# Linear attention and MLP on one core: k normalized inside its exponential, one ring of PSUM banks, casting loads for batch 0, earlier loads for the rest

## The chip, the cores and the metric

The kernel runs on one core of one Trainium2 chip. The metric is the time of one execution in microseconds on the device. Executions of one kernel mostly agree within 0.3%. A program on one core has no second die to compare with, so a run is called slow only when it lies over 1.5% above the fastest of the same kernel.

Names: PE is TensorE, PEld its weight loads, DVE is VectorE, ACT is ScalarE, POOL is GpSimd, SP is SyncE, which only issues transfers here. L599 is line 599 of that kernel's file, so line numbers differ between kernels.

## The reference

Attention with random features over 8 batches, 8 heads, 576 rows and head size 64, then an MLP over the 4608 rows:

```python
def phi(x):                                   # x is q or k, scaled by 64 ** -0.25
    proj = np.einsum('bhsd,md->bhsm', x, omega)
    h = proj - np.sum(x * x, axis=-1, keepdims=True) / 2.0
    h = h - np.max(h, axis=-1, keepdims=True)
    return np.exp(h) / np.sqrt(m)
kv = np.einsum('bhsm,bhsd->bhmd', k_p, v)
z = np.sum(k_p, axis=2)
out = np.einsum('bhsm,bhmd->bhsd', q_p, kv) / (np.einsum('bhsm,bhm->bhs', q_p, z)[..., None] + 1e-06)
# ... out to rows of 512, then
g = h * np.clip(h + 3.0, 0.0, 6.0) / 6.0      # h = x @ w_in   (512 x 2048)
return g @ w_out                              # 2048 x 512
```

The square term cancels inside the maximum. For q the maximum cancels in the division too. For k it does not: each row of k has to be weighted by exp(-its maximum).

## The kernel before

A small scheduler in the file decides, when the program is built, the order of the operations on every engine. It simulates the engines with a cost per operation (`occ`) that the author wrote in, takes the operations by priority, and then emits each engine's list with semaphore waits. At run time every engine executes its list in order. Two of the costs are

```python
    def actt(n):                  # ScalarE, n columns
        return 0.07 + n / 1200.0

    def dvet(n):                  # VectorE
        return 0.07 + n / 960.0
```

The MLP of block b-1 is placed beside the attention of batch b, so that TensorE always has large matmuls to do. The k side of the attention, for each of nine groups of four 128-column chunks per batch:

```python
            op("ACT", actt(512), lambda E, u=u, vK=vK: E.activation(
                kp[pb][:, 4 * u:4 * u + 4, :].rearrange("p c m -> p (c m)"), ring.t[vK.slot], AF.Exp, scale=alpha),
               pos(u) + 0.02, reads=[vK], writes=[("kp", pb, u)], name="eK%d.%d" % (b, u))
            op("DVE", dvet(512), lambda E, u=u: E.reduce_max(
                mx[pb][:, 4 * u:4 * u + 4], kp[pb][:, 4 * u:4 * u + 4, :], axis=AX.X),
               pos(u) + 0.03, reads=[("kp", pb, u)], writes=[("mx", pb, u)], name="mx%d.%d" % (b, u))
```

One exponential covers 512 columns. The maximum is taken from the result, its reciprocal `cc` is the row's weight, and v is multiplied by it (`vc`, and `vcl` for the left-over rows 512 to 575). The kv matmuls follow:

```python
        cbc = bass.AP(cc[pb], c0, [[NCH, 128], [1, 8], [0, D]])
        # ...
        op(EV_V if b else V0, {"POOL": 1.2, "DVE": dvet(512)}, lambda E: E.tensor_tensor(
            vcm[:, :, 0:D], v32[:, m, :, :], cbc, ALU.mult),
           t, reads=[("cc", pb, m), ("v32", 0, m), ("v32", 1, m)], writes=[("vc", u2, 0)], name="vc" + nm)
```

Two of the eight PSUM banks are kept for the numerators, six go round in a ring:

```python
    num_ps = P8[:, 0:2, :]
    ring = Ring([P8[:, i, :] for i in range(2, 8)])
```

Batch 0 is loaded in fp32 through SP and ACT and cast on the engines; later k and q are cast by the transfer itself, issued from POOL. Loads of batches 3 to 7 start at given steps of the MLP (16 steps per block):

```python
            load(0, ("SP", "ACT", "SP", "ACT"), {t: [] for t in "kqv"})
            # ...
            load(b, (), {"k": [("m1", b - 2, 10)], "q": [("m1", b - 2, 13)], "v": [("m1", b - 2, 15)]})
```

The softmax here doesn't subtract the row's maximum and nothing guards it: scores larger than these inputs give would overflow.

Of the kernel before, what the change touches and what calls it, by code (L numbers as in the profile page):

```python
# [13 lines left out]
EV0 = (("ACT","DVE"), ("ACT","DVE"), ("POOL","DVE"), {"k": ("POOL", "ACT", "DVE"), "q": ("POOL", "ACT","DVE")})  # L14
# [284 lines left out]
def _emit(nc, es, q, k, v, omega, w_in, w_out, out):  # L299
# [6 lines left out]
    NP = H // 2  # L306
# [8 lines left out]
    SPLIT = 3  # L315
    LATE = 0.4
    FIRST = [("k", 1), ("q", 1), ("k", 0), ("v", 0), ("v", 1), ("q", 0)]
    REST = [("k", 1), ("k", 0), ("q", 1), ("q", 0), ("v", 0), ("v", 1)]
    W_GATE = [("v32", 0, 1), ("v32", 0, 3), ("v32", 1, 3), ("v32", 1, 3)]
    alpha = float(D) ** -0.25  # L320
    PE_T, PE_X = 2, 2
    SPARE = 1
    EV_T = ("DVE", "ACT")
    EV_C = ("POOL", "ACT", "DVE")
    EV_V = ("POOL", "DVE")
    EV_L = ("POOL", "ACT")
    K0, T0, V0, C0 = EV0
# [9 lines left out]
    k32 = sbt("k32", [128, NCH, D], F32)  # L337
    q32 = sbt("q32", [128, NCH, D], F32)
    v32 = sbt("v32", [128, NP, 8, D], F32)
    vl = [sbt("vl%d" % u, [128, NP, D + 1], F32) for u in range(2)]  # L340
    kb = sbt("kb", [128, NCH, D], BF16)
    qb = sbt("qb", [128, NCH, D], BF16)
    half = k32[:].rearrange("p c d -> p (c d)").bitcast(BF16)
    KB = [kb, half[:, 0:NCH * D].rearrange("p (c d) -> p c d", d=D)]
    QB = [qb, half[:, NCH * D:2 * NCH * D].rearrange("p (c d) -> p c d", d=D)]
# [5 lines left out]
    cc = [sbt("cc%d" % u, [128, NCH], F32) for u in range(2)]  # L351
    vc = [sbt("vc%d" % u, [128, 520], BF16) for u in range(2)]
# [13 lines left out]
    om = sbt("om", [128, 2, M], BF16)  # L366
    ident = sbt("ident", [128, 128], BF16)
    ones = sbt("ones", [128, 8], F32)

    P8 = es.enter_context(nc.psum_tensor("p8", [128, 8, 512], F32))  # L370
    num_ps = P8[:, 0:2, :]
    ring = Ring([P8[:, i, :] for i in range(2, 8)])
# [36 lines left out]
    def turned(vx, b, n):  # L409
# [5 lines left out]
    op("POOL", 0.3, lambda E: E.memset(ident[:], 0.0), -9, writes=["ident"], lat=0.1)  # L415
    op("POOL", 0.4, lambda E: E.affine_select(out=ident[:], in_=ident[:], compare_op=ALU.not_equal, fill=1.0,
                                              base=0, pattern=[[-1, 128]], channel_multiplier=1),
       -9, reads=["ident"], writes=["ident"])
    op("DVE", 0.1, lambda E: E.memset(om[64:128, 0, :], 0.0), -9, writes=["omz0"])
    op("DVE", 0.1, lambda E: E.memset(om[0:64, 1, :], 0.0), -9, writes=["omz1"])  # L420
    for u in range(2):
        op("DVE", 0.2, lambda E, u=u: E.memset(vcl[u][:], 0.0), -8, writes=[("vcz", u)])
        op("DVE", 0.1, lambda E, u=u: E.memset(vl[u][:, :, D:D + 1], 1.0), -8, writes=[("vl1", u)])
    op("DVE", 0.1, lambda E: E.memset(ones[:], 1.0), -8, writes=["ones"])
    for i in range(2):
        op("DVE", 0.15, lambda E, i=i: E.tensor_copy(om2[:, i, :], om32[:]), -9, reads=["om32"],
           writes=[("om2", i)])
# [4 lines left out]
    op("DVE", 0.2, lambda E: E.tensor_copy(om[0:64, 0, :], ring.t[vom.slot][0:64, 0:M]), -9, reads=[vom],  # L432
       writes=["om0"])
    op("DVE", 0.2, lambda E: E.tensor_copy(om[64:128, 1, :], ring.t[vom.slot][64:128, 0:M]), -9, reads=[vom],
       writes=["om1"])
    omk = ["om0", "om1", "omz0", "omz1"]

# [4 lines left out]
    def w_in_piece(i, gate):  # L442
        f0, f1 = WI[i]
        op("POOL", 0.9 * (f1 - f0), lambda E: E.dma_start(
            wi[:, :, 128 * f0:128 * f1], w_in[:, 128 * f0:128 * f1].rearrange("(c p) f -> p c f", p=128)),
           -8.6 + 0.05 * i, reads=gate, writes=[("wi", i)], group="dwi%d" % i, inc=16, lat=2.0, name="wi%d" % i,
           issue=0.85, packet=91.0)

    def w_out_piece(g, gate):
        op("POOL", 3.6, lambda E: E.dma_start(  # L450
# [8 lines left out]
    def load(b, eng, gates):  # L459
        pb = b % 2  # L460
        halves = HALVES if b == 0 else [(0, NP)]
        turn_of = [0]

        def dma(part, dst, src, n, keys, gate, prio, run):
            cast = b > 0 and part[0] in "kq"
            e = "POOL" if cast else eng[turn_of[0]] if turn_of[0] < len(eng) else "SP"
            op(e, n * (0.78 if run == 1024 else 1.15) / 262144.0 * (1.08 if cast else 1.0),
               lambda E: E.dma_start(dst, src), prio + 0.001 * turn_of[0], reads=gate + (free if cast else []), writes=keys,  # L468
               group="d" + part + ("c" if cast else "") + (str(pb) if b and part != "v" else ""), inc=16, lat=1.9,
               name="%s.%d" % (part, b), issue=0.85 if cast else 0.47, packet=50.0 if run == 1024 else 18.0)  # L470
            turn_of[0] += 1


        free = [("kb", 0, x) for x in range(NDC)] if b == 1 else []

        def landing(t, hh, m0, m1):

            if t == "v" or b == 0:
                return [(t + "32", hh, m) for m in range(m0, m1)]
            return [(t + "b", pb, 2 + 4 * m + 2 * hh + x) for m in range(m0, m1) for x in range(2)]  # L480
# [3 lines left out]
        def mains(t, src, dst):  # L484
            for x, (m0, m1) in enumerate(halves):
# [7 lines left out]
        def lefts_of(t, hh):  # L493
            return [(t + "b", pb, x, hh) for x in range(2)]

        def lefts(t, src, dst):
            if t == "q":
                for hh in range(2):
                    dma("ql%d" % hh, dst[64 * hh:64 * hh + 64, 0:NP, :],
                        src[b, hh:H:2, MAIN:S].rearrange("m s d -> s m d"), 65536, [("q32l", hh)] if b == 0 else lefts_of(t, hh),  # L500
                        gates[t], base[t], 256)
            else:
                sap = src[b].rearrange("(m h) s d -> m (h s) d", h=2)[:, MAIN:MAIN + 128, :]
                dma(t + "l", vl[pb][:, :, 0:D] if t == "v" else dst[:, 0:NP, :],
                    sap.rearrange("m x d -> x m d"), 131072, [("vl", pb)] if t == "v" else [("k32l", 0)] if b == 0 else lefts_of(t, 0),
                    gates[t], base[t], 256)

        tensors = {"k": (k, KB[pb] if b else k32), "q": (q, QB[pb] if b else q32), "v": (v, v32)}
        for t, part in FIRST if b == 0 else REST:
            (mains if part else lefts)(t, *tensors[t])  # L510


    def attention(b):
# [7 lines left out]
        def left_keys(t):  # L521
            return [(t + "32l", hh) for hh in range(2 if t == "q" else 1)]

        def main_keys(t, ms, hs=(0, 1)):
            return [(t + "32", hh, m) for m in ms for hh in hs]

        def rows_of(t, dbl):

            if b == 0:
                return [(t + "b", 0, x) for x in dbl]  # L530
# [8 lines left out]

        def cast(t, name, n, dst, src, rd, dbl, p):  # L540
            op(EV_C if b else C0[t], {"POOL": 0.1 + n / 850.0, "ACT": actt(n), "DVE": 0.1 + n / 1500.0}, evac(lambda: dst, lambda: src),
               p, reads=rd, writes=[(t + "b", 0, x) for x in dbl], name="cast%s%d.%s" % (t, b, name))
# [25 lines left out]
        def pairs(t):  # L568
            return t[:, NP:, :].rearrange("p (j s c) d -> p j s (c d)", s=2, c=2)

        if b == 0:
            for m0, m1 in HALVES:
                for hh in range(2):
                    nm = "%d%d" % (m0 // 2, hh)
                    dbl = four(m0, m1, hh)
                    cast("k", nm, 512, mains_of(kb)[:, m0:m1, hh, :], mains_of(k32)[:, m0:m1, hh, :],
                         main_keys("k", range(m0, m1), [hh]), dbl, 0)
                    turns("k", nm, dbl, dbls(kT)[:, m0:m1, hh, :], kb, 0)
            for s in range(2):
                for m0, m1 in HALVES:  # L580
                    nm = "%d%s" % (m0 // 2, "AB"[s])
                    dbl = every(m0, m1, s)
                    cast("q", nm, 512, pairs(qb)[:, 2 * m0:2 * m1, s, :], pairs(q32)[:, 2 * m0:2 * m1, s, :],
                         main_keys("q", range(m0, m1)), dbl, 0)
                    turns("q", nm, dbl, alts(qT, s, m0, m1), qb, 0)
            for t, src, cst, dst in (("k", k32, kb, kT), ("q", q32, qb, qT)):
                late = 0 if t == "k" else LATE
                cast(t, "l", 256, flat(cst[:, 0:NP, :]), flat(src[:, 0:NP, :]), left_keys(t), [0, 1], late)
                turns(t, "l", [0, 1], dst[:, 0:2, :], cst, late)
# [4 lines left out]
        else:  # L594
            for t, cst, dst in (("k", KB[pb], kT), ("q", QB[pb], qT)):
                for i, (x0, x1) in enumerate(((0, 10), (10, 18))):
                    op("SP", 0.21 * (x1 - x0), lambda E, x0=x0, x1=x1, cst=cst, dst=dst: E.dma_start_transpose(
# [4 lines left out]
        for u in range(NU):  # L602
            vK = Virt(ring)

            def e_K(E, u=u, vK=vK):
                for i in range(2):
                    ins = E.matmul(ring.t[vK.slot][:, 256 * i:256 * i + 256], kT[:, 2 * u + i, :],  # L607
                                   om[:].rearrange("d t m -> d (t m)"), start=True, stop=True)
                return ins

            op("PE", 2 * mmt(256), e_K, pos(u) + 0.02, reads=[("kT", 2 * u), ("kT", 2 * u + 1)] + omk, writes=[vK],
               alloc=[vK], lat=0.25, slack=sl, spare=sp, name="K%d.%d" % (b, u))
            op("ACT", actt(512), lambda E, u=u, vK=vK: E.activation(  # L613
                kp[pb][:, 4 * u:4 * u + 4, :].rearrange("p c m -> p (c m)"), ring.t[vK.slot], AF.Exp, scale=alpha),
               pos(u) + 0.02, reads=[vK], writes=[("kp", pb, u)], name="eK%d.%d" % (b, u))
            op("DVE", dvet(512), lambda E, u=u: E.reduce_max(  # L616
                mx[pb][:, 4 * u:4 * u + 4], kp[pb][:, 4 * u:4 * u + 4, :], axis=AX.X),
               pos(u) + 0.03, reads=[("kp", pb, u)], writes=[("mx", pb, u)], name="mx%d.%d" % (b, u))
# [345 lines left out]
```

## Time and profile before

| | before |
|---|---|
| time, median of the 4 runs beside the changed kernel | 329.75 us (329.56 to 330.75) |
| span of the profiled run | 328.2 us |
| PE busy | 313.8 us, idle 14.4 us |
| first MLP matmul | 21.78 us |
| first MLP matmul of block 1 | 62.98 us |
| last matmul ends | 324.1 us |

A busy engine is one whose instructions cover the time. For PE this flatters: a 512-column matmul is shown as 379 ns long although four in a row take 0.86 us, that is 216 ns from start to start. A gap of up to 0.16 us between two matmuls is therefore hidden in "busy". The prediction below shows the rows of the page.

### The profile page before, as it was taken

How to read it: one execution, taken by the hardware profiler on the slowest of the kernel's cores; microseconds unless marked ns; L12 is line 12 of the kernel's file. 1: busy time of each engine (PE TensorE's matmuls, PEld its weight loads, DVE VectorE, ACT ScalarE, POOL GpSimd, SP SyncE). 2: the span in 40 equal slices, each digit the busy share in tenths (PEclk: the TensorE clock that was granted, in tenths of full speed). 3: DMA queues.
4: the chain of work that ended last, by engine and by line, in shares of the span. 5: the costliest groups of instructions: out<-in, count | busy, mean ns of one | idle time of the engine just before them, and what ended most of it. 6: DMA issues, size and time to landing. Idle time of an engine off the chain costs nothing.

```text
span 328.2 us, 5706 instructions
## 1 busy us (share of the span) xinstructions
PE 313.8 (96%) x2185; PEld 168.8 (51%) x2185; DVE 213.8 (65%) x421; ACT 181.6 (55%) x372; POOL 76.2 (23%) x108
## 2 busy tenths in 40 slices
PE   3699999999999999999999999999999999999994
PEld 2367865554655544545645544556545444444442
DVE  3858977489596951798768814986878373443311
ACT  3776975288696530796756403984686164344400
POOL 2835525008223230072130600361310000000000
PEclk9989999999999999999999999999999999999999
DMA  7999999959993299659890999099802101000033
GB/s 254 228 194 155 235 178 153 298 109 106 214 216 94 38 163 252 175 61 142 181 244 18 125 265 220 1 152 180 262 32 46 52 21 44 34 32 34 34 86 72
DMA packets 89356, 44.32 MB, mean 135 GB/s; under 512 B 56049, under 2 KB 84721, under 8 KB 89329
## 3 DMA queue, kind: packets, MB, share of 16 engines
q1 hardware_dynamic: 62272, 30.98, 40.1%
q0 software_dynamic: 26512, 12.46, 31.2%
q10 hardware_dynamic: 544, 0.52, 0.5%
q8 instruction: 17, 0.28, 0.4%
q14 instruction: 11, 0.08, 0.1%
HBM read 36.73 MB, written 9.44 MB: 141 GB/s over the span
## 4 chain that ended last, share of the span: by engine, by line
PE 88%; DMA 4%; DVE 3%; SPq 1%; ACT 1%; issue 1%; DVEq 0%
PE p L873 36%; PE p L818 34%; PE p L624 4%; PE p L607 4%; PE p L843 4%; PE p L751 3%; PE p L725 3%; DMA qT<-k 2%; DMA k<-in_k_dram 2%; SPq L468 1%; DVE mx L616 1%; PE p L407 1%; DVE gT L854 1%; PE p L727 1%; ACT qpT L628 1%
## 5 line engine op out<-in xcount | busy, mean ns | idle before, releaser
L873 PE MATMUL p<-wo,gT 128*128 128x512 bf16 x576 | 136.3, 379 | 0.3 <-ACT qpT L628 0.3
L824 ACT ACTIVATE tsb<-p 128x512 bf16<-128x512 f32 x128 | 76.8, 607 | 71.5 <-PE p L818 70.3
L826 DVE SCALAR_TENSOR_TENSOR gT<-tsb,p 128x512 bf16<-128x512 bf16 x128 | 86.1, 681 | 43.3 <-ACT tsb L824 42.8
L818 PE MATMUL p<-xT,wi 128*128 128x512 bf16 x448 | 103.9, 379 | 0.2 <-ACT qpT L628 0.2
L873 PEld LDWEIGHTS p<-wo,gT 128*128 128x128 bf16 x576 | 55.1, 98 | 60.6 <-ACT qpT L628 0.5
L818 PEld LDWEIGHTS p<-xT,wi 128*128 128x128 bf16 x448 | 42.9, 98 | 47.7 <-ACT qpT L628 0.9
L616 DVE TENSOR_REDUCE mx<-kp 128x4 f32<-128x512 bf16 x72 | 46.5, 668 | 3.3 <-ACT kp L613 3.2
L628 ACT ACTIVATE qpT<-p 128x512 bf16<-128x512 f32 (+1 forms) x80 | 41.1, 572 | 4.9 <-PE p L624 4.2
L613 ACT ACTIVATE kp<-p 128x512 bf16<-128x512 f32 x72 | 39.4, 625 | 3.1 <-PE p L607 3.1
L394 DVE COPY osb<-p 128x512 f32<-128x512 f32 x22 | 15.2, 692 | 38.3 <-PE p L873 38.2
L712 POOL TENSOR_TENSOR vc<-v,cc 128x512 bf16<-128x512 f32 x20 | 22.0, 1100 | 29.6 <-DVE cc L708 12.6
L767 DVE TENSOR_TENSOR xb<-p,rec 128x640 bf16<-128x640 f32 (+1 forms) x36 | 26.1, 729 | 0.3
L624 PE MATMUL p<-qT,om 128*128 128x512 bf16 (+1 forms) x80 | 23.9, 363 | 1.6 <-ACT qT L393 1.2
L607 PE MATMUL p<-om,kT 128*128 128x256 bf16 x144 | 23.0, 281 | 0.2
L647 POOL TENSOR_TENSOR vcl<-vl,cc 64x260 bf16<-64x260 f32 x10 | 6.2, 619 | 58.9 <-DVE cc L643 58.6
L607 PEld LDWEIGHTS p<-om,kT 128*128 128x128 bf16 x144 | 13.7, 100 | 7.4 <-DVE kT L394 0.9
L393 ACT COPY osb<-p 128x512 f32<-128x512 f32 x14 | 8.4, 603 | 16.0 <-PE p L873 16.0
L818 PE MATMUL p<-xS,wi 128*128 128x512 bf16 x64 | 16.4, 379 | 0.0
L751 PEld LDWEIGHTS p<-kvz,qpT 128*128 128x128 bf16 x312 | 13.7, 98 | 4.8 <-DVE kvz L394 0.4
L843 PE MATMUL p<-xT,wi 128*128 128x256 bf16 x128 | 15.5, 273 | 0.6 <-DVE xT L394 0.3
L725 PEld LDWEIGHTS p<-vc,kp 128*128 128x128 bf16 x256 | 12.1, 100 | 6.7 <-DVE vcl L647 1.4
L751 PE MATMUL p<-kvz,qpT 128*128 128x65 bf16 x312 | 15.3, 195 | 0.0
(72 smaller groups left out, 207.5 us busy)
## 6 DMA issues: line engine op xcount, KB each, us to landing
out_dram<-osb SPq DMA_DIRECT2D x32, 256.0 KB, 2.9
v<-in_v_dram SPq DMA_DIRECT2D x14, 512.0 KB, 6.9
wi<-in_moe_w_in_dram POOLq DMA_DIRECT2D x4, 512.0 KB, 8.1
k<-in_k_dram POOLq DMA_DIRECT2D x8, 256.0 KB, 4.4
k<-in_q_dram POOLq DMA_DIRECT2D x8, 256.0 KB, 5.5
wo<-in_moe_w_out_dram POOLq DMA_DIRECT2D x4, 512.0 KB, 9.9
kb<-in_k_dram POOLq DMA_DIRECT2D x6, 256.0 KB, 4.9
qb<-in_q_dram POOLq DMA_DIRECT2D x6, 256.0 KB, 6.1
```

The source lines that it names most:

```text
L607: ins = E.matmul(ring.t[vK.slot][:, 256 * i:256 * i + 256], kT[:, 2 * u + i, :], om[:].rearrange("d t m -> d (t m)"), start=True, stop=True)
L613: op("ACT", actt(512), lambda E, u=u, vK=vK: E.activation(kp[pb][:, 4 * u:4 * u + 4, :].rearrange("p c m -> p (c m)"), ring.t[vK.slot], AF ...
L616: op("DVE", dvet(512), lambda E, u=u: E.reduce_max(mx[pb][:, 4 * u:4 * u + 4], kp[pb][:, 4 * u:4 * u + 4, :], axis=AX.X), pos(u) + 0.03, r ...
L624: op("PE", mmt(n), lambda E, vQ=vQ, lh=lh: E.matmul(ring.t[vQ.slot][:, 0:n], om[:, lh, :], src, start=True, stop=True), p + 0.045 * lh, re ...
L628: op("ACT", actt(n), lambda E, vQ=vQ, lh=lh: E.activation(dst(lh), ring.t[vQ.slot][:, 0:n].rearrange("m (j t) -> m j t", t=128), AF.Exp, s ...
L751: ins = E.matmul(d[:, hh, i - i0, :], qpT[pb][:, o:o + 128], kvz[m][:, 65 * hh:65 * hh + 65], start=True, stop=True)
L767: op("DVE", dvet(128 * n), lambda E: E.tensor_tensor(xv[:, :, i0:i1, :], psum()[:, :, :, 0:64], rbc, ALU.mult), t + 0.01, reads=[key, ("re ...
L818: ins = E.matmul(ring.t[vh.slot], wi[:, c, 128 * f:128 * f + 128], xv[:, c, :], start=(c == 0), stop=(c == NJ - 1))
L824: op("ACT", actt(512), lambda E: E.activation(tsb[tu][:], ring.t[vh.slot], AF.Relu, bias=0.5, scale=1.0 / 6.0), t - 0.1, reads=[vh], write ...
L826: op("DVE", dvet(512), lambda E: E.scalar_tensor_tensor(gT[gu][:, f, :], tsb[tu][:], 1.0, ring.t[vh.slot], ALU.min, ALU.mult), t - 0.1, re ...
L843: ins = E.matmul(ring.t[vh.slot][:, 256 * g:256 * g + 256], wi[:, c, 128 * (f + g):128 * (f + g) + 128], xT[0][:, c, 256 * half:256 * half ...
L873: ins = E.matmul(ring.t[vo.slot], gT[gu][:, f, 128 * tc:128 * tc + 128], wo[:, f, :], start=(f == 0), stop=(f == NF - 1))
```

## The change

Its intent: let ScalarE apply the row weight of k for nothing, as the bias of the exponential, so that v needs only a cast and reciprocals and products go; use all banks for everything; let transfers do the casts of batch 0; and load later batches earlier, with a second buffer for v. The scores of k are computed negated (`omn`), so that a minimum out of PSUM is at once the bias. Smaller parts come with it: `vc` gets four buffers instead of two, the scale of k and q is folded into omega, the left-over rows of v are cast by their transfers, batch 0 is loaded in another order, and the scheduler's costs of loads and transposes are revised. The core of the diff, with cuts marked by three dots and two comments added:

```diff
-            op("ACT", actt(512), lambda E, u=u, vK=vK: E.activation(
-                kp[pb][:, 4 * u:4 * u + 4, :].rearrange("p c m -> p (c m)"), ring.t[vK.slot], AF.Exp, scale=alpha),
...
-            op("DVE", dvet(512), lambda E, u=u: E.reduce_max(
-                mx[pb][:, 4 * u:4 * u + 4], kp[pb][:, 4 * u:4 * u + 4, :], axis=AX.X),
...
+            op("DVE", dvet(512), lambda E, u=u, vK=vK: E.tensor_reduce(
+                mx[pb][:, 4 * u:4 * u + 4], ring.t[vK.slot].rearrange("p (c m) -> p c m", m=M), axis=AX.X, op=ALU.min),
...
+            for x in range(0, 4, EK):                                    # EK = 2
+                def e_exp(E, u=u, vK=vK, x=x):
+                    for i in range(x, x + EK):
+                        ins = E.activation(kp[pb][:, 4 * u + i, :], ring.t[vK.slot][:, M * i:M * i + M], AF.Exp,
+                                           bias=mx[pb][:, 4 * u + i:4 * u + i + 1], scale=-1.0)
+                    return ins
+                op("ACT", EK * actt(128), e_exp, pos(u) + 0.02, reads=[vK, ("mx", pb, u)],
...
-        op("DVE", 0.18, lambda E: E.reciprocal(cc[pb][:, c0:c0 + 8], mx[pb][:, c0:c0 + 8]), t,
...
-        op(EV_V if b else V0, {"POOL": 1.2, "DVE": dvet(512)}, lambda E: E.tensor_tensor(
-            vcm[:, :, 0:D], v32[:, m, :, :], cbc, ALU.mult),
...
+        op(EV_V if b else V0, {"POOL": 0.1 + 512 / 850.0, "ACT": actt(512), "DVE": 0.1 + 512 / 1500.0},
+           evac(lambda: vcm[:, :, 0:D], lambda: v32[pb][:, m, :, :]), t - 0.03,
...
-    num_ps = P8[:, 0:2, :]
-    ring = Ring([P8[:, i, :] for i in range(2, 8)])
+    ring = Ring([P8[:, i, :] for i in range(8)])
...
-        tail([0, 1], 0, 5, True)
+        tail([0], 0, 3)
+        tail([1], 3, 5)
...
-            load(0, ("SP", "ACT", "SP", "ACT"), {t: [] for t in "kqv"})
+            load(0, {"k": [], "q": [], "v": [V_GATE]})       # k, q and left-over v cast by POOL's transfers; V_GATE: the left-over k
...
-            load(b, (), {"k": [("m1", b - 2, 10)], "q": [("m1", b - 2, 13)], "v": [("m1", b - 2, 15)]})
+            load(b, {"k": [("m1", b - 2, 2)], "q": [("m1", b - 2, 5)], "v": [("m1", b - 2, 8)]})
```

A bias is one value per partition, and each 128-column chunk has its own. So a group now needs four exponentials of 128 columns where one of 512 was enough.

## The prediction

> **What bounds the kernel now.** I read first the busy time of each engine on the page, then a table of windows along the span, then the timeline of the start, and last the groups of instructions split by shape. The page says that TensorE is the bound:
>
> ```profile
> PE 313.8 (96%) x2185; PEld 168.8 (51%) x2185; DVE 213.8 (65%) x421; ACT 181.6 (55%) x372; POOL 76.2 (23%) x108
> ```
>
> The span is 328.2 us, so PE is idle for 328.2 - 313.8 = 14.4 us. The windows (start and end; busy us and instructions of PE, PE weight loads, VectorE, ScalarE, GpSimd; granted clock; DMA share; GB/s) say where:
>
> ```profile
> 0.00:4.00 4.00, 0.29 (x1) 0.10 (x1) 1.42 (x11) 1.28 (x1) 0.89 (x7) 1.00 0.50 156
> 4.00:8.00 4.00, 2.57 (x19) 1.75 (x20) 1.57 (x5) 1.50 (x3) 1.02 (x2) 1.00 1.06 348
> 8.00:12.00 4.00, 3.08 (x28) 2.27 (x26) 2.77 (x8) 2.75 (x6) 2.45 (x4) 1.00 1.17 310
> 12.00:16.00 4.00, 1.93 (x18) 0.79 (x16) 3.92 (x9) 3.62 (x8) 3.77 (x5) 1.00 0.89 154
> 16.00:20.00 4.00, 3.70 (x51) 2.69 (x50) 3.04 (x11) 3.26 (x11) 3.11 (x4) 0.57 1.20 180
> 20.00:24.00 4.00, 3.77 (x41) 2.69 (x38) 1.87 (x7) 2.90 (x8) 0.00 (x0) 1.00 1.24 206
> ...
> 36.00:40.00 4.00, 4.00 (x47) 3.67 (x46) 3.97 (x10) 4.00 (x10) 2.31 (x5) 1.00 1.11 186
> ```
>
> PE is busy 15.34 us of the first 24, so 8.66 us of the idle time lie there. Some 4.1 us lie after the last matmul at 324.1 (output copy and store). That leaves 14.4 - 8.7 - 4.1 = 1.6 us for the 300 us between. A wider window, 63 to 98 us, has PE busy 35.00 of 35, and four 512-column matmuls take 0.86 us in the chain, 0.216 us each. So after 24 us nothing is to be had except by less PE work, and the change removes none: scores, projections, kv, numerators, transposes and both MLP matmuls stay in number and shape. Only the start can pay, and the rest can only lose. The timeline of the start:
>
> ```profile
> 4.22 0.51 SPq L468 DMA_DIRECT2D k<-in_k_dram  x1
> ...
> 8.82 2.56 ACT L613 ACTIVATE kp<-p 128x512 bf16<-128x512 f32 x5 [0.62 <-PE p L607]
> ...
> 10.63 0.29 DVE L394 CAST kb<-k 128x256 bf16<-128x256 f32 x1 [1.22 <-DMA k<-in_k_dram]
> ...
> 14.86 0.95 DVE L647 TENSOR_TENSOR vcl<-vl,cc 64x260 bf16<-64x260 f32 x2
> ...
> 15.87 0.40 PEld L725 LDWEIGHTS p<-vc,kp 128*128 128x128 bf16 x8 [1.35 <-DVE vcl L647]
> ...
> 21.78 0.83 PE L843 MATMUL p<-xT,wi 128*128 128x256 bf16 x6
> ...
> 26.74 2.73 POOL L468 DMA_DIRECT2D k<-in_q_dram  x4 [0.23 <-DMA wi<-in_moe_w_in_dram]
> ```
>
> The left-over rows of k are issued at 4.22 and their cast waits until 10.63; VectorE then needs 5.2 us of maxima, reciprocals and products until the first kv matmul at 15.87; the first MLP matmul is at 21.78. The last piece of w_in has landed at 26.7, just as PE has used the other twelve sixteenths (48 of 64 matmuls by 27.0). So the start has two limits close together, the chain through VectorE and ScalarE, and the loads.
>
> **What the Trainium skill says.** "ScalarE: Activation LUTs", What ACT_TABLE_LOAD costs, gives an ACTIVATE with immediate scale and bias 186 ns + 0.833 ns per column, a per-partition pointer operand 93 ns more, and an overlap of 93 ns back to back. The trace agrees on the first: 512 columns give 612 ns against 620 measured; five in 2.56 us are (2.56 - 0.62)/4 = 0.485 us apart, a bit closer than 612 - 93 = 519. No instruction of this trace has a pointer bias. "VectorE: DVE Perf Modes", The perf-mode tier table, says that a reduction runs at 1x wherever its source lies; the trace has 668 ns for the 512-column maximum out of SBUF and 692 for a 512-column copy out of PSUM, so the new minimum out of PSUM should cost the same. "DMA: Bandwidth & Descriptors", SWDGE vs HWDGE vs iDMA, says that a cast in a DMA must be issued from GpSimd, whose software writes the descriptors and takes longer to set up; here a GpSimd issue takes 0.7 to 0.8 us against 0.47 on SP. "TensorE: Matmul & The Clock Gate", What's actually happening, has the clock at half after a quiet 3.4 us window; the 0.57 in 16 to 20 us, after 12 to 16 with PE busy 1.93 of 4, agrees in kind.
>
> **The change part by part.** The rows by shape that I count with:
>
> ```profile
> L616 DVE TENSOR_REDUCE mx<-kp 128x4 f32<-128x512 bf16 x72 | 46.5, 668 | 3.3 <-ACT kp L613 3.2
> L613 ACT ACTIVATE kp<-p 128x512 bf16<-128x512 f32 x72 | 39.4, 625 | 3.1 <-PE p L607 3.1
> L767 DVE TENSOR_TENSOR xb<-p,rec 128x640 bf16<-128x640 f32 x28 | 22.9, 819 | 0.3
> L712 DVE TENSOR_TENSOR vc<-v,cc 128x512 bf16<-128x512 f32 x12 | 9.5, 792 | 0.7 <-issue 0.7
> L708 DVE RECIPROCAL cc<-mx 128x8 f32<-128x8 f32 x32 | 6.2, 194 | 0.3
> L763 DVE RECIPROCAL rec<-p 128x10 f32<-128x10 f32 x28 | 6.0, 216 | 3.9 <-PE p L751 3.9
> L716 ACT CAST vc<-cc 128x8 bf16<-128x8 f32 x24 | 5.5, 238 | 1.0 <-DVE cc L708 0.9
> ```
>
> ScalarE, exponentials of k: one 512-column instruction becomes four of 128 with a pointer bias. By the page one takes 280 + 107 = 387 ns, and 387 - 93 = 294 ns from start to start (estimate from that page). Four make 1.18 us against 0.49, so +0.69 us on each of nine groups, +6.2 us per batch, +50 us in all; minus 5.5 us of small copies. ScalarE goes from 182 to some 226 us, 69% of the span: no bound on average.
>
> VectorE: reciprocals of the maxima go (6.2 + 1.2 us), of the products on v 9.5 us become casts at the 427 ns of a 512-column cast (12 x 0.43 = 5.1), the left-over products go (3.0). The numerator in two parts adds 28 more reciprocals (28 x 0.17 = 4.8) and turns 819 ns into about 550 + 415 (28 x 0.15 = 4.1). Sum -7.4 - 4.4 - 3.0 + 8.9 = -6 us, nothing that PE waits for. GpSimd loses 22.0 us of products against some 12 of casts, and is idle most of the time anyway.
>
> At the start: no casts for k and q, so VectorE loses 0.72 us, ScalarE 0.62 and GpSimd the rest; k is issued by GpSimd one after another at 0.8 us, so the first piece lands perhaps 0.7 us later than the 3.8 of now and is ready when its cast ended before (4.4); the fourth is no earlier. The left-over k comes fifth, issued at about 4.5 and landed near 8.5 instead of 10.6: 2 us gained on that chain. VectorE does five reciprocals (about 1 us), two left-over products (0.95) and one or two products on v (0.7 each) less before the MLP. But ScalarE now owes 9 x 1.18 = 10.6 us of exponentials from about 6.8, thus not before 17.4, plus the four projections of q that the first half needs (4 x 0.5 = 2.0): 19.4 with no gap and no copies at all. The last pair then still has kv, its copy, numerator, division, transpose and copy to go: about 3 us from the trace's own rows, part of which overlaps the projections of q. That puts the first MLP matmul at 20.5 to 22, against 21.8: a gain of 0 to 1.3 us. A fuller PE between 12 and 16 us could also avoid the half-clock stretch, worth at most (3 x 0.5 + 0.2) = 1.7 us of PE time; I count half a microsecond.
>
> Loads: the same bytes read from HBM. Cast loads move 200 GB/s written, 400 read, against some 350 for plain ones, so 2.36 MB of k and q come 0.8 us sooner at best (estimate from the windows); the gates of w_in still hang on v, and v now waits for the left-over k. I take w_in within 1 us of now.
>
> Eight banks in one ring, the second v buffer, the earlier gates: they attack waits that PE barely has. The two that can be seen are 0.34 us near 42 and 0.37 us near 169 (a late load of k, q or v); I give this 0.5 us.
>
> Sum: start -0.7, clock -0.5, loads -0.5, stalls -0.5, and +0.6 for new stalls (next paragraph): -1.6 us, so 328.0.
>
> **The rivals.** First, ScalarE becomes the bound at the start and in batch 1. For it: it is 4.00 of 4 us busy at 36 to 40 us, VectorE 3.97, and 6 us more come on top where the MLP of block 0 runs beside the attention of batch 1. The rows of batch 1 must be done before block 1 at 63 us; against it, ScalarE is busy only 4.73 of 13 us from 50 to 63. If it bites: 330 to 333. Second, the start is bound by the loads: then an earlier first matmul only moves the wait to the last piece of w_in or to w_out, and the time stays at 329 to 330. Third, the VectorE chain was the true limit and the scheduler hides the exponentials: the MLP starts at 18 to 19 and w_in keeps up, 325 to 326. The hard limit is PE: even without any of the 8.7 us at the start the first k has to land, about 5 us, so more than 4 us of gain is hardly possible; 2% would be 6.6.
>
> **Range and chances.** From the rivals 324.5 to 331.5. Faster by over 2% needs more than the idle time offers, 0.04; slower by over 2% (over 336.2) needs stalls in every one of seven blocks, for which a steady PE with 6 us more of ScalarE work in 35 gives little reason, 0.03.
>
> **What would show it.** In the profile after: PE busy again 311 to 315 us; exponentials of k x288 at about 0.39 us; ScalarE near 225 us; no reciprocals of the maxima; first MLP matmul between 20.5 and 22; w_in landed at 25.7 to 27; idle PE after 24 us under 2.5 us. Wrong would be: a first MLP matmul under 19.5 us, a last w_in before 25, PE gaps behind the exponentials in each block, or exponentials much cheaper than 0.39 us.

## The result, and the profile after

The changed kernel took 341.6 us (340.95 to 342.33, 4 runs) against 329.75 us: 3.5% slower, where 328.0 had been predicted with 331.5 as the upper end. Ratios here are the mean time of one kernel's fast runs over that of the other's of the same rounds, so they are not quite the ratio of the medians quoted: here 1.0353, with a 95% interval of 1.0323 to 1.0384.

The page of the changed kernel, busy time of each engine and then the chain that ended last by engine:

```profile
PE 318.4 (94%) x2185; PEld 167.9 (49%) x2185; DVE 209.3 (62%) x444; ACT 211.6 (62%) x559; POOL 70.3 (21%) x106
...
PE 70%; ACT 14%; DMA 9%; DVE 3%; POOL 1%; issue 1%; SPq 0%; POOLq 0%
```

PE has the same 2185 matmuls and is idle 339.5 - 318.4 = 21.1 us instead of 14.4. ScalarE, which was 1% of the chain before, is 14% of it now, although it is busy only 62% of the span. The groups of instructions by shape (line, engine, operation, output<-input, shape, count | busy us, mean ns | idle before them and what ended it) of the changed kernel:

```profile
L599 ACT ACTIVATE kp<-p,mx 128x128 bf16<-128x128 f32 x288 | 82.6, 481 | 30.7 <-DVE mx L593 30.6
L793 ACT ACTIVATE tsb<-p 128x512 bf16<-128x512 f32 x128 | 81.9, 684 | 59.1 <-PE p L787 58.4
L593 DVE TENSOR_REDUCE mx<-p 128x4 f32<-128x512 f32 x72 | 46.1, 684 | 6.2 <-PE p L587 5.8
```

The exponentials of k fill 82.6 us where they filled 39.4. The minimum out of PSUM costs 684 ns against 668 for the maximum, as expected. The timeline shows how the exponentials lie (start, length; "x28" is a run of 28 back to back):

```profile
21.67 0.83 PE L812 MATMUL p<-xT,wi 128*128 128x256 bf16 x6
...
28.05 2.73 POOL L473 DMA_DIRECT2D qb<-in_q_dram  x4 [0.31 <-DMA wi<-in_moe_w_in_dram]
...
165.10 7.34 ACT L599 ACTIVATE kp<-p,mx 128x128 bf16<-128x128 f32 x28 [4.79 <-DVE mx L593]
...
172.49 0.31 PEld L696 LDWEIGHTS p<-vc,kp 128*128 128x128 bf16 x8 [0.81 <-ACT kp L599]
```

They come in a burst, because the k of a whole batch is transposed by two transfers. Twenty-eight of them hold ScalarE from 165.1 to 172.4, and at 172.49 the kv matmuls of PE have waited for them. ScalarE had been idle for 4.79 us just before. The same thing in a window of the steady part, first before, then after (window, then busy us and count of PE, PE weight loads, VectorE, ScalarE, GpSimd, then clock, DMA share, GB/s):

```profile
66.00:261.00 195.00, 194.63 (x1368) 102.12 (x1367) 141.95 (x270) 117.14 (x246) 48.81 (x65) 1.00 0.79 140
```

```profile
66.00:261.00 195.00, 189.61 (x1317) 97.30 (x1315) 133.96 (x278) 139.47 (x385) 38.96 (x57) 1.00 0.89 140
```

In the same 195 us PE is idle 5.39 us instead of 0.37, and gets 51 matmuls less done. ScalarE does 139 us in 195, and that is enough to stall PE.

The start went differently from what was expected too. The windows of the changed kernel that answer to those of the kernel before:

```profile
0.00:4.00 4.00, 0.26 (x1) 0.10 (x1) 1.58 (x16) 1.28 (x1) 2.59 (x9) 1.00 0.37 43
4.00:8.00 4.00, 3.04 (x19) 1.67 (x20) 3.60 (x10) 0.81 (x4) 3.99 (x6) 1.00 1.09 117
8.00:12.00 4.00, 3.35 (x19) 2.29 (x18) 2.73 (x7) 2.50 (x10) 1.85 (x3) 1.00 1.31 185
...
36.00:40.00 4.00, 3.16 (x34) 2.77 (x33) 2.86 (x5) 3.50 (x12) 2.99 (x4) 1.00 1.26 267
```

The GB/s of a casting load count what is written, half of what is read: the DMA view lists a quarter of the main rows of k with 128 KB here and with 256 KB before. Even doubled, 43 and 117 are 86 and 234 GB/s read, against 156 and 348 before. The DMA view of the first 9 us, before and then after:

```profile
DMA packets 3036, 2.31 MB, mean 256 GB/s; under 512 B 995, under 2 KB 3036, under 8 KB 3036
```

```profile
DMA packets 1941, 0.72 MB, mean 80 GB/s; under 512 B 736, under 2 KB 1941, under 8 KB 1941
```

At most 1.44 MB had been read by 9 us, against 2.31 MB, so the loads stand at least 0.87 MB behind. At the 350 GB/s of the kernel before that is 2.5 us (an estimate from these windows). The loads behind them are late: the q of batch 1, which goes out when the last piece of w_in has landed, at 28.05 against 26.74; the first w_out at 36.3 against 34.6. Up to 40 us the chain that ended last runs through loads nearly all the way: k of batch 0, v (which its gate holds until 9.03 us), w_in, then k and v of batch 1. The first MLP matmul is at 21.67, as before, but PE is then idle 0.84 us in the window from 36 to 40, which was full.

| | before | after | later by |
|---|---|---|---|
| first MLP matmul | 21.78 | 21.67 | -0.1 |
| first MLP matmul of block 1 | 62.98 | 65.67 | 2.7 |
| last matmul ends | 324.1 | 335.4 | 11.3 |

So some 3 us are lost between 22 and 66 us, and 8.6 us after that.

### The profile page after: what moved, and what is told of

It is laid out like the page before. It is cut to its first block, busy times and chain, and to the rows that moved or that the text cites. A ratio compares the mean times of both kernels' runs of the same rounds, so it can differ in the third digit from the quotient of the medians.

```text
span 339.5 us, 5858 instructions
## 1 busy us (share of the span) xinstructions
PE 318.4 (94%) x2185; PEld 167.9 (49%) x2185; DVE 209.3 (62%) x444; ACT 211.6 (62%) x559; POOL 70.3 (21%) x106
## 3 DMA queue, kind: packets, MB, share of 16 engines
q0 software_dynamic: 34080, 14.16, 39.4%
## 4 chain that ended last, share of the span: by engine, by line
PE 70%; ACT 14%; DMA 9%; DVE 3%; POOL 1%; issue 1%; SPq 0%; POOLq 0%
PE p L842 32%; PE p L787 29%; ACT kp L599 12%; DMA v<-in_v_dram 4%; PE p L610 3%; DMA wi<-in_moe_w_in_dram 3%; DMA kb<-in_k_dram 3%; PE p L719 2%; PE p L696 2%; ACT tsb L793 1%; DVE mx L593 1%; POOL kb L473 1%; ACT qpT L614 1%; PE p L587 1%; DVE osb L392 1%
## 5 line engine op out<-in xcount | busy, mean ns | idle before, releaser
L793 ACT ACTIVATE tsb<-p 128x512 bf16<-128x512 f32 x128 | 81.9, 684 | 59.1 <-PE p L787 58.4
L787 PE MATMUL p<-xT,wi 128*128 128x512 bf16 x448 | 107.5, 379 | 1.8 <-ACT kp L599 1.4
L599 ACT ACTIVATE kp<-p,mx 128x128 bf16<-128x128 f32 x288 | 82.6, 481 | 30.7 <-DVE mx L593 30.6
L787 PEld LDWEIGHTS p<-xT,wi 128*128 128x128 bf16 x448 | 42.2, 98 | 49.9 <-ACT kp L599 2.8
L593 DVE TENSOR_REDUCE mx<-p 128x4 f32<-128x512 f32 x72 | 46.1, 684 | 6.2 <-PE p L587 5.8
L614 ACT ACTIVATE qpT<-p 128x512 bf16<-128x512 f32 (+1 forms) x80 | 48.0, 739 | 1.4 <-PE p L610 1.4
L473 POOL DMA_DIRECT2D kb<-in_k_dram x26 | 19.5, 761 | 88.7 <-PE p L787 73.5
L735 DVE TENSOR_TENSOR xb<-p,rec 128x384 bf16<-128x384 f32 (+1 forms) x64 | 29.0, 477 | 0.1
L392 POOL CAST vc<-v 128x512 bf16<-128x512 f32 x18 | 12.4, 687 | 54.6 <-DMA v<-in_v_dram 49.5
L587 PE MATMUL p<-omn,kT 128*128 128x256 bf16 x144 | 23.2, 290 | 0.2 <-ACT kp L599 0.2
L473 POOL DMA_DIRECT2D qb<-in_q_dram x32 | 21.9, 701 | 3.4 <-PE p L787 2.1
L587 PEld LDWEIGHTS p<-omn,kT 128*128 128x128 bf16 x144 | 14.5, 104 | 8.7 <-ACT kp L599 1.1
L787 PE MATMUL p<-xS,wi 128*128 128x512 bf16 x64 | 16.4, 379 | 0.0
L696 PEld LDWEIGHTS p<-vc,kp 128*128 128x128 bf16 x256 | 11.6, 98 | 9.4 <-ACT kp L599 4.3
```

Source lines behind the costliest of these rows:

```text
L392: return E.tensor_copy(dst(), src())
L473: lambda E: E.dma_start(dst, src), prio + 0.001 * turn_of[0], reads=gate, writes=keys,
L587: ins = E.matmul(ring.t[vK.slot][:, 256 * i:256 * i + 256], kT[:, 2 * u + i, :], omn[:].rearrange("d t m -> d (t m)"), start=True, stop=True)
L593: op("DVE", dvet(512), lambda E, u=u, vK=vK: E.tensor_reduce(mx[pb][:, 4 * u:4 * u + 4], ring.t[vK.slot].rearrange("p (c m) -> p c m", m=M ...
L599: ins = E.activation(kp[pb][:, 4 * u + i, :], ring.t[vK.slot][:, M * i:M * i + M], AF.Exp, bias=mx[pb][:, 4 * u + i:4 * u + i + 1], scale= ...
L614: op("ACT", actt(n), lambda E, vQ=vQ, lh=lh: E.activation(dst(lh), ring.t[vQ.slot][:, 0:n].rearrange("m (j t) -> m j t", t=128), AF.Exp), ...
```

## The experiments

Theory A: the four narrow exponentials with a bias column make ScalarE so much slower in the attention phases that PE waits for it. Theory B: it is less the work than the order, because the scheduler was told 0.177 us for one exponential where the trace shows about 0.26. Rivals: the shared ring of banks, the earlier loads, the splitting into four as such, and for the start the casting loads or the gate on v.

Two of the twelve kernels give a wrong result, which is said there. All others are correct. The kernel before ran beside each group: median 329.24 for the first two groups, 328.89 for the third, 329.6 for the last.

### e1_wide: two exponentials of 256 columns, no bias

```diff
-                    for i in range(x, x + EK):
-                        ins = E.activation(kp[pb][:, 4 * u + i, :], ring.t[vK.slot][:, M * i:M * i + M], AF.Exp,
-                                           bias=mx[pb][:, 4 * u + i:4 * u + i + 1], scale=-1.0)
-                    return ins
+                    return E.activation(kp[pb][:, 4 * u + x:4 * u + x + EK, :].rearrange("p c m -> p (c m)"),
+                                        ring.t[vK.slot][:, M * x:M * x + M * EK], AF.Exp, scale=-1.0)
```

> The changed kernel in exactly its own order on every engine, but each group of k takes two 256-column exponentials with no bias instead of four of 128 columns with one (wrong result on purpose: k is not normalized). Theory A, the narrow exponentials with a bias overload ScalarE in bursts and TensorE waits behind them: the exponentials of one group fall from about 1.05 us to about 0.55 us, and the time comes down from 341.6 to 331 to 335. Rivals (the shared bank ring, the earlier loads, the order itself): the time stays at 339 to 342.

Measured: 330.85 us (330.45 to 334.95), ratio to before 1.0078 (1.0018 to 1.0139). The order on PE, DVE, POOL and SP is that of the changed kernel. 10.7 of the 11.9 us are gone with nothing but shorter exponentials. Ring, gates and order are the same, so none of them loses these 10.7 us by itself.

### e3_nobias: four exponentials of 128 columns, no bias

```diff
-                                           bias=mx[pb][:, 4 * u + i:4 * u + i + 1], scale=-1.0)
+                                           scale=-1.0)
```

> The changed kernel in its own order, four exponentials of 128 columns per group as before but with no bias column (wrong result on purpose). It splits theory A in two: if the per-partition bias is what costs, one exponential goes from 0.26 us start to start to about 0.2 and the time to 335 to 338; if the splitting in four alone costs, the time stays within 1 us of 341.6.

Measured: 332.3 us (331.38 to 333.84), ratio 1.0085 (1.0059 to 1.0111). This is the whole of the splitting, and it costs at most 1.5 us over e1_wide. The bias column alone costs 9.3 us in this order, more than I expected. The burst at the same place of the order, in the timeline of this run:

```profile
161.68 5.07 ACT L599 ACTIVATE kp<-p 128x128 bf16<-128x128 f32 x28 [4.79 <-DVE mx L593]
```

The same 28 exponentials take 5.07 us instead of 7.34. With the last one's own length taken off (0.35 and 0.48 us, the mean of the group), the starts are (5.07 - 0.35)/27 = 0.175 us apart without a bias and (7.34 - 0.48)/27 = 0.254 with one. That is 79 ns for the bias. Times 288 it is 23 us of ScalarE, of which 9.3 reach the end.

The dose matters. Per group of four chunks the scheduler was told 4 x 0.177 = 0.71 us. The real groups take about 0.59 us in e1_wide (two at 0.30), 0.70 in e3_nobias and 1.02 in the changed kernel. The two at or below what the scheduler was told are within 1.5 us of each other; the one above it loses 9.3 us more. That points to theory B.

### e2_cost: the scheduler is told the truth

```diff
-                op("ACT", EK * actt(128), e_exp, pos(u) + 0.02, reads=[vK, ("mx", pb, u)],
+                op("ACT", EK * 0.262, e_exp, pos(u) + 0.02, reads=[vK, ("mx", pb, u)],
```

> The changed kernel with right results; only the static scheduler is told that a narrow exponential costs 0.262 us, as the trace shows, instead of 0.177, so the orders change. If the loss is a schedule made with a wrong cost (theory B): 330 to 336. If the loss is that ScalarE has too much to do in the attention phases whatever the order (theory A in its hard form): 338 to 342.

Measured: 335.01 us (332.83 to 336.8), ratio 1.0174 (1.0118 to 1.0230). The same instructions in another order, and 6.6 us come back. So more than half of the loss was an order made for exponentials that do not exist, and theory B holds for that part. The four runs lie 4 us apart, which the runs of the kernel before do not, so the 6.6 is good to 2 us or so. The window of the steady part, of the profiled run, which was the fastest of the four:

```profile
66.00:261.00 195.00, 193.25 (x1343) 102.48 (x1368) 139.00 (x281) 144.38 (x395) 39.39 (x58) 1.00 0.83 139
```

Some matmul records are missing from this trace (2149 of 2185), so the weight loads are the count to go by: 1368, as before (1367), against 1315 in the changed kernel. The first MLP matmul of block 1 starts at 65.2 us, 2.2 later than before, and the last matmul ends at 326.9, 2.8 later. So in this run 0.6 us are lost after block 1 began, where the changed kernel lost 8.6. In this run the order alone mends the steady part; what is left lies before it.

### e4_before_narrow: the kernel before, with narrow biased exponentials

```diff
# ... zero: four columns of zeros, set once at the start
-            op("ACT", actt(512), lambda E, u=u, vK=vK: E.activation(
-                kp[pb][:, 4 * u:4 * u + 4, :].rearrange("p c m -> p (c m)"), ring.t[vK.slot], AF.Exp, scale=alpha),
...
+            def e_exp(E, u=u, vK=vK):
+                for i in range(4):
+                    ins = E.activation(kp[pb][:, 4 * u + i, :], ring.t[vK.slot][:, M * i:M * i + M], AF.Exp,
+                                       bias=zero[:, i:i + 1], scale=alpha)
+                return ins
...
+            op("ACT", actt(512), e_exp,
...
```

> The kernel before in its own order, with each 512-column exponential of k cut in four of 128 columns whose bias is a column of zeros (right result). Theory A: it becomes slower by 5 to 12 us, to 335 to 342, with TensorE idle behind the exponentials. If the other parts of the change carry the loss: 329 to 332.

Measured: 355.78 us (355.47 to 356.65), ratio 1.0812 (1.0793 to 1.0831). The direction is that of theory A, but it is over twice what I expected. ScalarE has 80 - 39 = 40 us more to do, and 26 of them reach the end. From the waits of this run (who waited for what: us in total, times, longest):

```profile
PEld p L631 <- ACT kp L617: 10.8, 13, 0.9
PEld p L825 <- ACT kp L617: 9.9, 12, 1.0
...
PEld p L609 <- ACT kp L617: 6.7, 16, 1.0
```

L631, L825 and L609 are the projections of q, the MLP and the scores of k: not consumers of these exponentials but matmuls that need the bank that they hold. So the harm in the kernel before is larger than in the changed kernel (26 against 12 us). Two reasons are possible. Its scheduler was told 0.50 us for a group that takes 1.02 (32 exponentials in 8.38 us at 174.46), a gap of 0.52 where the changed kernel has 0.31; or other parts of the change make up for some of the harm. No run separates the two.

### e6_late_gates: the later loads back

```diff
-            load(b, {"k": [("m1", b - 2, 2)], "q": [("m1", b - 2, 5)], "v": [("m1", b - 2, 8)]})
+            load(b, {"k": [("m1", b - 2, 10)], "q": [("m1", b - 2, 13)], "v": [("m1", b - 2, 15)]})
```

> The changed kernel (right result) with the loads of batches 3 to 7 gated at MLP steps 10, 13 and 15 as before, not 2, 5 and 8. If the earlier loads help, as meant: 343 to 346. If they cost by colliding with stores and transposes: 337 to 340. Theory A (neither matters, the exponentials do): 340.5 to 343.

Measured: 353.22 us (350.94 to 353.91), ratio 1.0715 (1.0672 to 1.0758). The earlier loads are worth 11.6 us in the changed kernel. The window of the steady part, and in another view who waited longest for the exponentials, both of this run:

```profile
66.00:261.00 195.00, 182.40 (x1237) 92.12 (x1236) 126.92 (x256) 129.72 (x366) 37.92 (x55) 0.98 0.81 134
```

```profile
PEld p L696 <- ACT kp L599: 13.4, 10, 1.9
PE p L696 <- ACT kp L599: 10.3, 10, 1.8
PEld p L787 <- ACT kp L599: 8.1, 12, 1.0
```

PE is idle 12.6 us in these 195 instead of 5.4. The kv matmuls (L696) and the MLP (L787) stand behind the exponentials. It is not that late loads crowd the exponentials of one batch together: in this trace they lie within 18.8 and 9.6 us by turns, against 10.9 to 15.3 in the changed kernel. But the batches themselves come unevenly, at 73.2, 99.6, 148.8, 175.3, 224.2 and 250.7 us, where the changed kernel has them 25 to 38 us apart. Whether that unevenness is the cause was not tested. The early gates may be what made up for part of the harm that e4_before_narrow showed.

### e8_own_banks: six banks in the ring, two for the numerators

```diff
-    ring = Ring([P8[:, i, :] for i in range(8)])
+    num_ps = P8[:, 0:2, :]
+    ring = Ring([P8[:, i, :] for i in range(2, 8)])
...
-        tail([0], 0, 3)
-        tail([1], 3, 5)
+        tail([0, 1], 0, 5, True)
```

> The changed kernel (right result) with the banks as before: six in the ring and two kept for the numerators of batches 1 to 7, whose reciprocal and division are one instruction again. If the shared ring helps against the long-held banks of k: 345 to 355. If splitting the numerators costs: 338 to 340. Theory A expects it slower than 341.6, since a group of k now holds its bank for minimum and exponentials, near 1.8 us.

Measured: 342.19 us (341.64 to 343.03), ratio 1.0395 (1.0367 to 1.0422). That is the changed kernel's time within its spread. The ring of eight is neither the cause nor a help here. My expectation that six banks would be clearly slower was wrong.

### e5_v_early: v of batch 0 not gated

```diff
-            load(0, {"k": [], "q": [], "v": [V_GATE]})
+            load(0, {"k": [], "q": [], "v": []})
```

> The changed kernel (right result) with one gate undone: the loads of the first v no longer wait for the left-over rows of k, so they go out on SP from the first microsecond beside the casting loads. Theory A for the start: the loads of the change begin too thin (234 GB/s read in 4 to 8 us against 348 before) and everything behind them, the last piece of w_in at 28.0 and w_out at 36.3 us, comes 1.3 to 1.7 us late; then w_in lands near 26.5 and the time falls by 1.5 to 3 us, to 338.5 to 340. Rival: the start is not bound by the loads, and the time stays within 1 us of 341.6, or rises because v takes the bandwidth from k.

Measured: 344.26 us (342.47 to 345.5), ratio 1.0437 (1.0398 to 1.0476), slower, not faster. In its trace the first score matmul of k starts at 8.7 us against 5.8 and the first MLP matmul at 25.3 against 21.7. With v in flight too, the four pieces of k take 5.4 us (median) from issue to landing instead of 3.2. So the gate on v is not the fault; it protects the casting loads of k.

### e7_hybrid: all of the change but the treatment of k and v

Scores with `om`, one exponential of 512 columns, maximum, reciprocals and products on v as before. Casting loads, ring of eight, second v buffer and early gates as in the change.

> Everything of the change except the treatment of k and v: 512-column exponentials without bias, then maximum, reciprocal and the product on v, as before, with the casting loads, the ring of eight banks, the second v buffer and the earlier gates of the change (right result). Theory A: 329 to 333, all the loss but that of the start is gone. If ring and gates bring the gain that was meant, 323 to 328. If they carry part of the loss: 334 or more.

Measured: 331.89 us (331.15 to 333.67), ratio 1.0087 (1.0050 to 1.0124). So the treatment of k and v carries 341.6 - 331.9 = 9.7 us of the change. The first MLP matmul of block 1 starts at 66.0 us, 3.0 later than before, and the last matmul ends 3.7 later: what this kernel loses, it loses at the start. (The profiled run is the slowest of its four, 333.67 us.) There PE waits for k of batch 1 (start, length, and in brackets the idle time before and its cause):

```profile
34.00 0.73 PE L407 MATMUL p<-ident,kb 128*128 128x128 bf16 x10 [2.22 <-DMA kb<-in_k_dram]
```

The granted clock then shows 0.83 and 0.74 in the windows from 32 to 36 and 36 to 40 us, where it was 1.00 in the kernel before. Its DMA view of the first 9 us reads like that of the changed kernel:

```profile
DMA packets 2010, 0.75 MB, mean 83 GB/s; under 512 B 736, under 2 KB 2010, under 8 KB 2010
```

### e9_before_early, e10_before_ring, e11_before_both: gates, ring, and both, put into the kernel before

```diff
# e9 and e11: second buffer v32[pb] wherever v32 was used, and ...
-            load(b, (), {"k": [("m1", b - 2, 10)], "q": [("m1", b - 2, 13)], "v": [("m1", b - 2, 15)]})
+            load(b, (), {"k": [("m1", b - 2, 2)], "q": [("m1", b - 2, 5)], "v": [("m1", b - 2, 8)]})
# e10 and e11, with the reads of the numerators widened to match ...
-    num_ps = P8[:, 0:2, :]
-    ring = Ring([P8[:, i, :] for i in range(2, 8)])
+    ring = Ring([P8[:, i, :] for i in range(8)])
-        tail([0, 1], 0, 5, True)
+        tail([0], 0, 3, False)
+        tail([1], 3, 5, False)
```

> The kernel before with one part of the change alone: loads of batches 3 to 7 gated at MLP steps 2, 5, 8 and v double buffered (right result). With 512-column exponentials ScalarE has room and TensorE is idle only 1.6 us between 24 and 324 us, so theory A expects no more than that: 327.5 to 330. If earlier loads are worth as much here as in the changed kernel (353.2 with late gates, 341.6 with early ones): 318 to 322.

> The kernel before with the one ring of eight banks alone, the numerators in two parts (right result). Theory A: 328.5 to 331, as the same edit was worth nothing in the changed kernel (342.2 without, 341.6 with). If the ring is a gain that the exponentials hid: 324 to 327.

> The kernel before with ring, early gates and second v buffer together (right result). Against the hybrid (331.9) it differs in the loads of batch 0 alone, plain on SP and ACT with casts on the engines here, casting loads from GpSimd there. If the casting loads cost the start 2 to 3 us, as the DMA rates say (0.72 MB written, thus some 1.35 MB read, in the first 9 us, against 2.31 MB): 327 to 330, at least 2 us under the hybrid. If the hybrid lost its time to the ring or the gates: 331 to 333.

Measured: e9_before_early 331.61 us (331.31 to 333.0), ratio 1.0083 (1.0059 to 1.0106); e10_before_ring 329.11 us (327.86 to 329.91), ratio 0.9992 (0.9968 to 1.0016); e11_before_both 328.61 us (328.03 to 329.82), ratio 0.9984 (0.9960 to 1.0008). Neither the ring nor both together move the time. The early gates alone, with the second v buffer, cost 2.7 us, against the expectation, and why the ring takes that back was not looked into: the whole order is made anew each time, which may move a kernel by as much, and no run tests that by itself.

e11_before_both loads batch 0 and the left-over rows of v plainly, where e7_hybrid casts them in the transfer, and it is 3.3 us faster. That is not the only difference, as the expectation has it: e7_hybrid also gates v, has four `vc` buffers instead of two, the scale folded into omega, another order of the first loads and other scheduler costs for loads and transposes. e11_before_both had moved 2.32 MB in its first 9 us:

```profile
DMA packets 3040, 2.32 MB, mean 258 GB/s; under 512 B 983, under 2 KB 3040, under 8 KB 3040
```

PE is busy 4.00 of 4 us there from 32 to 36 us, and the first w_out goes out at 33.8 us against 36.9 in e7_hybrid. So the casting loads, with their gate and these smaller parts, cost 3.3 us; the wait for k of batch 1 shows late loads at work, but that all of the 3.3 is theirs is not shown. Gates and ring together cost nothing.

### e12_both_mended: the change's arithmetic with both costs mended

The changed kernel with `EK * 0.262` as in e2_cost, and k and q of batch 0 through SP and ACT in fp32 with casts on the engines as before, v ungated; the order of the first loads goes back with them. The minimum, the biased exponentials, the cast-only v, ring and gates are those of the change.

> The change with its two suspected costs mended and its arithmetic kept (right result): the scheduler is told 0.262 us for a biased exponential, and k and q of batch 0 are loaded plainly through SP and ACT and cast on the engines as before, with v not gated. If the two costs are separate and add up: 335.0 - 3.3 = 331.7, within 330 to 333.5; what is left over 328.6 is then the price of the longer exponentials themselves. If they overlap (the start hides behind ScalarE anyway): 334 to 336. If nothing else is lost in the change: 328 to 330.

Measured: 332.88 us median of all six runs (331.12 to 336.38); two of the six were slow and stay out of the ratio, 1.0077 (1.0048 to 1.0106). The mean of the four fast runs is 332.3. The two costs add up, within the spread. Against e2_cost (1.0174, 1.0118 to 1.0230) it differs only in the loads of batch 0 and their casts, so this pair tests them more cleanly than the last one did, and gives the same 3 us. Its window of the steady part, and two windows of its start:

```profile
66.00:261.00 195.00, 195.00 (x1374) 102.87 (x1373) 138.61 (x281) 144.16 (x397) 38.46 (x56) 1.00 0.86 141
```

```profile
16.00:20.00 4.00, 2.75 (x32) 1.90 (x33) 1.86 (x6) 4.00 (x16) 1.01 (x2) 0.64 1.21 192
20.00:24.00 4.00, 4.00 (x41) 2.97 (x39) 3.41 (x13) 3.47 (x10) 0.39 (x1) 0.50 1.24 206
```

PE has not a gap in the 195 us, although ScalarE does even more in them than in the changed kernel (144.2 against 139.5 us). With an order made for their true length, the long exponentials cost nothing shown in the steady part. What is left, some 3 us over the kernel before, lies before 66 us, and its cause is open. The first MLP matmul is at 25.5 us, and the trace offers three causes for what is left. The exponentials: ScalarE is busy 4.00 of 4 us from 16 to 20. The clock: 0.64 and then 0.50 from 16 to 24 us, where the kernel before had 0.57 and then 1.00. And the loads: the chain that ended last runs through them up to 61 us, and at 62.4 PE has stood idle for 1.5 us behind work that waited for v. No run separates these.

No kernel tried is faster than the kernel before by more than the noise.

## Why the prediction was wrong

The account of the 11.9 us that the runs give: 9.7 for the treatment of k and v (e7_hybrid), of which 6.6 come back when the scheduler is told the right cost (e2_cost); 3.3 for the casting loads and the small parts beside them (e7_hybrid against e11_before_both); ring and early gates together nothing (e11_before_both). The 9.7 and 3.3 are steps along one row of kernels, from 328.6 over 331.9 to 341.6, so that they add up proves nothing. The check is in the other runs: 9.3 and 10.7 for the exponentials by e3_nobias and e1_wide, in the changed kernel's own order, and some 3 for the loads by e12_both_mended against e2_cost.

**"ScalarE goes from 182 to some 226 us, 69% of the span: no bound on average."** This step failed, and with it the dismissal of the first rival. The size was not the error: the measured 211.6 us and 0.254 us from start to start are even less than the 226 and 0.294 that I worked out. The error was to judge engines that run fixed orders by an average share. In e4_before_narrow 26 us of some 40 us of added ScalarE work reached the end, with ScalarE busy 62% of the span. The prediction never set two numbers side by side: the diff tells the scheduler `EK * actt(128)`, which is 0.177 us per exponential, and my own estimate was 0.294. An order built on a cost that is too low stalls wherever the exponentials come in a burst. (What counted was the measured 0.254 against the 0.177; the gap to my estimate was wider still.) I put +0.6 us for new stalls; 8.6 us were lost after block 1 began, and 0.6 in the profiled run of e2_cost. The first rival had been put at 330 to 333, and the range kept of that only what lies up to 331.5.

**"Slower by over 2% needs stalls in every one of seven blocks, for which a steady PE with 6 us more of ScalarE work in 35 gives little reason."** The stalls did come in the blocks, for the reason above. The chance of 0.03 was far too low.

**"So 2.36 MB of k and q come 0.8 us sooner at best", and "I take w_in within 1 us of now".** This failed too. I took the rate of casting loads from windows in which w_in was loaded. At the start the casting loads of k and q read 234 GB/s at most, and no more than 1.44 MB in 9 us. The last w_in was 1.3 us late and w_out 1.7, and the casting loads as a whole cost 3.3 us. The second rival had the right mechanism, that the start is bound by the loads, but I read it as a limit on the gain and not as a possible loss.

**The first MLP matmul "at 20.5 to 22".** Right: 21.67, but partly by luck. ScalarE was the limit there as worked out, busy 4.00 of 4 us from 12 to 16 and from 16 to 20. The exponentials were shorter than estimated, yet the last of them ended at 20.4 and not 17.4, because ScalarE had gaps at first and did projections of q in between. It brought no gain, since the loads behind it were late. The half-clock stretch was gone in the profiled run, as was hoped (1.00 from 16 to 20 us against 0.57), without a visible gain either.

**VectorE and GpSimd.** Mechanism right, size near: VectorE 213.8 to 209.3, -4.5 against -6, and nothing waited for it; the minimum at 684 ns against "the same" 668.

**"Eight banks in one ring, the second v buffer, the earlier gates: they attack waits that PE barely has."** Right for the kernel before: e11_before_both is the same as before. In the changed kernel it was wrong for the gates: without them it is 11.6 us slower (e6_late_gates), and TensorE waits longer for the exponentials; why is open.

**What was named as proof of a wrong prediction** came about: "PE gaps behind the exponentials in each block". PE's idle time after 24 us was 339.5 - 24 - (318.4 - 15.2) - 4.1 = 8.2 us, not under 2.5.

**What stays open.** Why the early gates alone cost 2.7 us in the kernel before and save 11.6 in the changed one, how much of every difference of some 3 us is the order made anew, and what the last 3 us of e12_both_mended are. No run takes the casting loads apart into the time of their issue from GpSimd (0.7 to 0.8 us each, one after another) and the rate of their packets. The DMA views speak for the packets: in the first 9 us they took 75% of the time of the 16 DMA engines for at most 1.44 MB read, in the kernel before 83% for 2.31 MB. At the rate of the kernel before, 75% would have been 2.1 MB (an estimate from these views).

## What to carry to other kernels

Where the orders are fixed when the program is built, an engine's average share says little: put the scheduler's cost of each changed instruction beside the duration that the trace shows, and expect stalls where the real one is longer and they come in bursts. A per-partition bias is not free on ScalarE (79 ns each here), and here the wide exponential followed by a product on another engine was better than the biased one. Before replacing plain loads at the start by casting ones, compare what each has read in the first microseconds, since everything loaded later stands in line behind them.

## What the Trainium skill lacked or had wrong

- "ScalarE: Activation LUTs", What ACT_TABLE_LOAD costs: its 93 ns for a pointer operand is 79 ns here from start to start (0.254 against 0.175 us for 128 columns out of PSUM), and 130 ns in the mean length shown. The lengths are off for such short ones: 481 ns is the mean shown with a bias and 351 without, where the page's terms give 387 and 293, and neighbours overlap by about 481 - 254 = 227 and 351 - 175 = 176 ns, not 93. Nor does a length shown stay fixed: the 512-column ReLU of the MLP, untouched by the change, has a median of 597 ns in both kernels, but its mean went from 607 to 684.
- "DMA: Bandwidth & Descriptors", SWDGE vs HWDGE vs iDMA: it says that casting loads must come from GpSimd and that setup there is slower, but has no figure for what a row of them brings at the start of a kernel. Here they had written 0.72 MB, so read at most 1.44, by 9 us, where plain loads through SP and ACT had moved 2.31 MB; over the whole kernel they cost, with the small parts that came with them, 3.3 us.
- No page gives a size for what ScalarE, far below full occupancy, costs TensorE when its instructions take longer than a fixed order allows for: with ScalarE busy 62% of the span, 79 ns on each of 288 instructions cost 9.3 us.
